# Four block-mean products in one go, 512 KB value loads, weight halves decoded in pairs, and a stage's scores in one TensorE run

## The chip, the cores and the metric

The kernel runs on one core of a Trainium2 chip. The metric is the time of one execution on the device in microseconds. The engines are called PE (TensorE, matrix products), PEld (its weight loads), DVE (VectorE), ACT (ScalarE), POOL (GpSimd) and SP (SyncE, which here issues every DMA).

## The reference

Attention in which each query sees a narrow window of keys and, beside it, one maximum of keys and one mean of values for each block of 32 positions; its result goes through a feed-forward net (FFN).

```python
# q, k, v: (B, H, S, D) = (4, 8, 768, 64); block 32, window 16; d_ff = 2048
k_sum = k.reshape(B, H, nb, block, D).max(axis=3)
v_sum = v.reshape(B, H, nb, block, D).mean(axis=3)
scores_l = where(|i - j| < window, q @ k.T / sqrt(D), -1e9)
scores_s = q @ k_sum.T / sqrt(D) + log(block)
a = softmax(concat(scores_l, scores_s))          # 1e-9 added to the sum
x = a @ concat(v, v_sum)                         # -> (B * S, H * D) = (3072, 512)
h = x @ w_in
out = (h / (1 + exp(-h))) @ w_out
```

## The kernel before

The 3,072 rows are cut into 24 attention stages of 128 rows (six for each batch) and 12 FFN chunks of 256 rows (two stages each). A chunk `c` goes through 16 slices `f` of the hidden width: `ffn1` (4 products), a tanh on ACT and a product on DVE, `ffn2` (2 outputs, `u` = 0, 1). Chunk 0 and batch 0's attention run in 32-bit floats, where one product is two passes of PE; all else is split into high and low 16-bit halves and takes three 16-bit products for one.

A planner (`Plan`) sets the order of everything. The code below registers each operation with its cost on each engine it may run on, with what it reads and writes, and with a priority; the planner sweeps over them, picks engine and place, and the program is issued in that order, engine by engine. `TUNE` holds the priorities' offsets. Where the planner sees PE idle at the start it puts in filler products (`fill`). Each engine runs its list strictly in order, so an instruction that waits holds up all behind it.

What the change and the prediction's steps touch:

- `job_qk`, `job_k0`: SP loads queries and keys (for batch 0 into `first` and `second`).
- `job_mean`: the block means of batch 0's values. For each of six tiles of 128 rows SP loads two halves `z` (120 and 96 rows of 512 columns, `v` 0 to 5, four of them into weight tiles `wr` not yet in use, two into `v0`); 12 products with a 0-or-1/32 matrix `sums` add up into 24 rows of one PSUM bank; that is copied to `vms`, and from there into the 24 free rows of each half tile.
- `job_a`: scores of a head group `m` (four for a stage; two of them share a run of products, `pair`), softmax with row maxima, exponentials and sums, and for batch 0 a transpose on PE (`turn`), for later batches a DMA transpose.
- `job_c`, `job_x`: the products of weights and values into bank 7, and its copy to `x`, the FFN's input.
- `job_load`, `job_w`: a weight slice comes as two loads (`kind` 0 of `w_in`, 1 of `w_out`) of 512 KB; ACT (`Prelu`), ACT or DVE (`last_bits`) and DVE turn its 64-bit words into 32-bit floats, and DVE takes the largest (`wm`).
- `w_scale`, `job_pair`: one scale for all weights, and each weight half as two 16-bit halves (`wh`, `wl`), which chunks 1 to 11 use.
- `job_f`: the FFN of a chunk and slice.

Score products write PSUM banks 2 to 5 at first and 6 and 3 later (`score_banks`).

Of the kernel before, what the change touches and what calls it, by code (L numbers as in the profile page):

```python
# [47 lines left out]
SETTLED = 32  # L48
SLACK = {"pe": 2500, "dve": 800, "act": 800, "pool": 800}
# [6 lines left out]
class Plan:  # L56
# [17 lines left out]
    RUSH = 140000  # L74

# [5 lines left out]
    def op(self, engines, fn, r=(), w=(), prio=0.0, cols=0, port=("dve", "pool"), fill=None):  # L81
# [11 lines left out]
        self.ops.append((engines, fn, sorted(deps), prio, cols, port, fill, dict(self.slack)))  # L93
# [20 lines left out]
    def sweep(self, prio, on, back):  # L114
# [9 lines left out]
        ready, seen, fills, filled, early, order = {}, {}, 0, self.FIRST, True, []  # L124
# [8 lines left out]
        while ready:  # L133
# [13 lines left out]
            if e == "pe" and not back:  # L147
# [8 lines left out]
                stop = self.stream(seen, t, cost, cols)  # L156
# [61 lines left out]
def local_attn_ffn(ctx: ExitStack, tc: tile.TileContext, qkT, qF, kF, v, vR, w, out):  # L218
# [15 lines left out]
    wp = ctx.enter_context(tc.tile_pool(name="wp", bufs=2 * NFT))  # L234
# [5 lines left out]
    wr = [wp.tile([P, 2 * DM], U32, name="wr") for _ in range(2 * NFT)]  # L240
# [5 lines left out]
    sums = const.tile([P, 2, NB + 4 * NTILE - 2], F32, name="sums")  # L246
    nc.vector.memset(sums, 0.0)
    for z in range(2):
        two, top = sums[:, z, NB - 2:NB], HALO + (0 if z else NB)
        nc.vector.memset(two, 1.0 / BLK)  # L250
        nc.gpsimd.affine_select(out=two, in_=two, pattern=[[-BLK, 2]], compare_op=ALU.is_ge, fill=0.0, base=-top, channel_multiplier=1)
        nc.gpsimd.affine_select(out=two, in_=two, pattern=[[BLK, 2]], compare_op=ALU.is_ge, fill=0.0, base=top + BLK - 1, channel_multiplier=-1)
    lg = const.tile([P, 1], F32, name="lg")
# [16 lines left out]
    NRAW, NP, NTT, NE, NG, NT2 = 3, 8, 12, 3, 4, 4  # L270
# [33 lines left out]
    sum_t = ring(3, [P, 2], F32, "sum")  # L304
# [30 lines left out]

    def both_ends(k):
# [34 lines left out]
    def job_scale(b, prio):  # L371
        prio += nudge("scale", b)
        for j in range(3):
            stg, key = staging()
            qf = stg[:, :2 * DM]
            plan.op({"dma": 1650}, lambda e, qf=qf, j=j: nc.sync.dma_start(out=qf, in_=qF[b - 1, :, j, :]), w=key, prio=prio)
# [9 lines left out]
        plan.op({"pe": 220}, tr, r=["qm_q", "qm_k"], w=[("bank", k)], prio=prio, cols=256)  # L386
# [29 lines left out]
    def v_scale(b, prio):  # L416
        k = sbank()
        plan.op({"pe": 110}, lambda e, k=k: nc.tensor.transpose(out=bank[k][:1, :P], in_=am_t[:, 7:8], identity=ident), r=["am4"], w=[("bank", k)], prio=prio, cols=128)
# [18 lines left out]
    def job_v(b, prio):  # L437
        prio += nudge("v", b)
        for j in range(4):
            stg, key = staging()  # L440
            vr = stg[:, :S]
            plan.op({"dma": 1230}, lambda e, vr=vr, j=j: nc.sync.dma_start(out=vr, in_=vR[b, :, j, :]), w=key, prio=prio)
# [6 lines left out]
        def tr(e, k=k):  # L449
# [10 lines left out]
    def job_qk(s, prio):  # L460
# [11 lines left out]
        plan.op({"dma": 1850}, lambda e: nc.sync.dma_start(out=raw4, in_=qkT[b, t]), w=key, prio=prio)  # L472
# [20 lines left out]
    def job_mean(prio):  # L493
        prio += nudge("mean")
        k = sbank()
        for t in range(NTILE):
            src, keys, _ = main0(t)
            for z in range(2):
                plan.op({"dma": 650}, lambda e, src=src, t=t, z=z: nc.sync.dma_start(out=src[rows0[z], z], in_=v[0, t, rows0[z], z, :]), w=[keys[z]], prio=prio)
        for t in range(NTILE):  # L500
            src, keys, _ = main0(t)
            for z in range(2):
                at = NB - 2 - 4 * t - 2 * z
                plan.op({"pe": 900}, lambda e, src=src, t=t, z=z, at=at, k=k: nc.tensor.matmul(out=bank[k][:NB], lhsT=sums[rows0[z], z, at:at + NB], rhs=src[rows0[z], z], start=(t == 0 and z == 0), stop=(t == NTILE - 1 and z == 1)),  # L504
                        r=[keys[z]], w=[("bank", k)], prio=prio, cols=2048)
# [417 lines left out]
```

## Time and profile before

| | |
|---|---|
| median of 3 runs | 617.32 us (616.46 to 617.68) |
| the profiled execution | 616.48 us |
| its span, first to last instruction | 614.4 us |
| mean granted TensorE clock | 0.997 |
| busy PE / DVE / ACT / POOL | 603.8 / 462.7 / 380.3 / 97.1 us |
| moved by DMA | 75.65 MB, mean 123 GB/s |

The time of an execution is 2.1 us more than its span. In the views of the profile a row of the timeline is: start, length, engine, line, operation, what it writes and reads, how many were merged, and in brackets how long the engine stood before it and what ended that. PE's products are pipelined, so a product's length is longer than the pitch at which products follow one another. In the view of groups the numbers behind the bar are the busy time and the mean ns of one.

### The profile page before, as it was taken

To read this page: it belongs to the slowest core of one execution; us is meant where nothing else is said; L and a number is where in the kernel's file an instruction comes from. 1 tells how busy PE (TensorE), PEld (TensorE's weight loads), DVE (VectorE), ACT (ScalarE), POOL (GpSimd) and SP (SyncE) were. 2 spreads that over 40 slices of the span, in tenths; PEclk is the share of its full clock that TensorE was granted. 3 is DMA by queue.
4 is the path that set the end of the run, shared out by engine and by line. 5 is a ranking of instruction groups with operands and counts; after the bars stand their busy time and mean duration, and the time that the engine had idled before them with its cause. 6 is when DMAs were issued, how large, how long until landed. Compare 5 with 4: busy or idle time off the path is not lost.

```text
span 614.4 us, 15092 instructions
## 1 busy us (share of the span) xinstructions
PE 603.8 (98%) x5648; PEld 398.1 (65%) x5648; DVE 462.7 (75%) x1517; ACT 380.3 (62%) x1049; POOL 97.1 (16%) x136
## 2 busy tenths in 40 slices
PE   7989999999999999999999999999999999999997
PEld 4366666666666666666666666666666666666664
DVE  4599999998997674997889965998856768833332
ACT  3799959986765664665665764655755565533333
POOL 3220000122414202004113300102123101100000
PEclk9999999999999999999999999999999999999999
DMA  9999344313733663363425761552722502200000
GB/s 236 322 400 409 136 125 123 118 49 105 197 85 76 181 194 51 113 163 101 130 60 126 185 194 33 112 161 70 180 66 38 173 19 41 71 10 1 35 1 34
DMA packets 66354, 75.65 MB, mean 123 GB/s; under 512 B 41978, under 2 KB 48122, under 8 KB 66282
## 3 DMA queue, kind: packets, MB, share of 16 engines
q1 hardware_dynamic: 66282, 74.70, 42.6%
q8 instruction: 44, 0.72, 0.5%
q14 instruction: 28, 0.23, 0.1%
HBM read 57.18 MB, written 6.29 MB: 103 GB/s over the span
## 4 chain that ended last, share of the span: by engine, by line
PE 95%; ACT 2%; SPq 1%; DVE 1%; DMA 1%; issue 0%
PE bank L747 38%; PE bank L755 38%; PE bank L744 5%; PE bank L752 5%; PE bank L577 4%; PE bank L651 2%; PE bank L504 2%; PE bank L636 1%; PE bank L609 1%; DMA wr<-in_v_dram 1%; SPq L362 1%; ACT wr L224 0%; DVE second L474 0%; ACT e L586 0%; PE bank L451 0%; PE bank L430 0%
## 5 line engine op out<-in xcount | busy, mean ns | idle before, releaser
L747 PE MATMUL bank<-x,wr 128*128 128x256 f16 x2112 | 258.1, 273 | 0.0
L747 PEld LDWEIGHTS <-wr 128*128 128x128 f16 x2112 | 204.8, 98 | 55.7 <-issue 0.9
L755 PE MATMUL bank<-wr,gh 128*128 128x512 f16 x704 | 209.9, 380 | 0.0
L761 ACT ACTIVATE t<-bank,th 128x256 f32<-128x256 f32 x176 | 82.9, 471 | 124.2 <-PE bank L747 123.9
L762 DVE SCALAR_TENSOR_TENSOR t<-t,bank 128x256 f32<-128x256 f32 x192 | 80.1, 418 | 87.7 <-ACT t L761 86.3
L755 PE MATMUL bank<-wr,gl 128*128 128x512 f16 x352 | 133.4, 379 | 0.0
L764 ACT ACTIVATE gh<-t 128x256 f16<-128x256 f32 x176 | 72.6, 414 | 58.9 <-DVE t L762 53.8
L765 DVE SCALAR_TENSOR_TENSOR gl<-t,gh 128x256 f16<-128x256 f32 x176 | 80.9, 461 | 33.7 <-ACT gh L764 32.8
L755 PEld LDWEIGHTS <-gh 128*128 128x128 f16 x704 | 65.0, 98 | 45.4 <-issue 0.3
L586 ACT ACTIVATE e<-e,mx 128x120 f32<-128x120 f32 x192 | 73.3, 386 | 4.6 <-DVE mx L583 4.0
L755 PEld LDWEIGHTS <-gl 128*128 128x128 f16 x352 | 34.4, 98 | 41.9 <-DVE gl L765 0.5
L620 DVE SCALAR_TENSOR_TENSOR first<-e,sum,first 128x120 f16<-128x120 f32 x144 | 47.7, 377 | 0.1
L583 DVE CUSTOM_DVE_ANT_0 e<-bank,masks,qsc 128x120 f32<-128x120 f32 x144 | 41.7, 337 | 0.3 <-PE bank L577 0.3
L586 ACT ACTIVATION_READ_ACCUMULATOR e<-e,mx 128x1 f32 x192 | 36.8, 192 | 0.0
L752 PE MATMUL bank<-wr,t 128*128 128x512 f32 x64 | 31.2, 602 | 0.0
L744 PE MATMUL bank<-x,wr 128*128 128x256 f32 x128 | 30.6, 383 | 0.3 <-ACT x L224 0.3
L744 PEld LDWEIGHTS bank<-x,wr 128*128 128x128 f32 x128 | 23.8, 190 | 7.7 <-issue 3.3
L231 POOL TENSOR_TENSOR first<-raw,first 128x1024 f16<-128x1024 f32 x13 | 28.2, 2174 | 0.9
L598 POOL TENSOR_SCALAR e<-e,sum 128x120 f32<-128x120 f32 x24 | 10.1, 427 | 111.3 <-DVE sum L591 103.1
L598 POOL TENSOR_SCALAR first<-e,sum 128x120 f16<-128x120 f32 x26 | 13.5, 522 | 82.2 <-DVE sum L591 40.5
L226 POOL TENSOR_SCALAR first<-raw 128x1024 f16<-128x1024 f32 x12 | 14.1, 1176 | 77.5 <-PE bank L651 77.3
L600 DVE TENSOR_SCALAR first<-e,sum 128x120 f16<-128x120 f32 x91 | 23.8, 288 | 0.8
(145 smaller groups left out, 642.6 us busy)
## 6 DMA issues: line engine op xcount, KB each, us to landing
wr<-in_w_dram SPq DMA_DIRECT2D x32, 512.0 KB
raw<-in_qkT_dram SPq DMA_DIRECT2D x18, 576.0 KB
raw<-in_v_dram SPq DMA_DIRECT2D x18, 512.0 KB
out_dram<-raw SPq DMA_DIRECT2D x24, 256.0 KB
raw<-in_kF_dram SPq DMA_DIRECT2D x12, 384.0 KB
raw<-in_qF_dram SPq DMA_DIRECT2D x9, 512.0 KB
raw<-in_vR_dram SPq DMA_DIRECT2D x12, 384.0 KB
first<-in_qkT_dram SPq DMA_DIRECT2D x6, 320.0 KB
```

Of the source, the lines that this page charges most:

```text
L231: eng[e].tensor_tensor(out=out, in0=in0, in1=in1, op=ALU.subtract)
L583: plan.op({"dve": 262 if b else 206}, lambda e, i=i: nc.vector.tensor_tensor_reduce(out=et[:, i, :], in0=sc[:, i, :NKEY], in1=mask, scale= ...
L586: plan.op({"act": 385}, lambda e, i=i: nc.scalar.activation(out=et[:, i, :], in_=et[:, i, :], func=AF.Exp, scale=-1.0, bias=mx[:, i:i + 1] ...
L620: nc.vector.scalar_tensor_tensor(out=pt[:, i, P:P + NKEY], in0=et[:, i, :], scalar=su[:, i:i + 1], in1=pt[:, i, :NKEY], op0=ALU.mult, op1= ...
L744: nc.tensor.matmul(out=h, lhsT=wi.bitcast(F32)[:, ct * P:(ct + 1) * P], rhs=x0[:, ct, :], start=(ct == 0), stop=(ct == NCT - 1))
L747: nc.tensor.matmul(out=h, lhsT=wip[:, part, ct * P:(ct + 1) * P], rhs=x[:, ct, :], start=(ct == 0 and q == 0), stop=(ct == NCT - 1 and q = ...
L752: nc.tensor.matmul(out=bank[ob[u]], lhsT=t[:, u * P:u * P + P], rhs=wo.bitcast(F32), start=opens, stop=closes)
L755: nc.tensor.matmul(out=bank[ob[u]], lhsT=g[:, u * P:u * P + P], rhs=wop[:, part, :], start=(opens and q == 0), stop=(closes and q == 2))
L761: plan.op({"act": 264 if c == 0 else 360}, lambda e: nc.scalar.activation(out=t, in_=h, func=AF.Tanh, scale=0.5 if c == 0 else th[:, 0:1]) ...
L762: plan.op({"dve": 337}, lambda e: nc.vector.scalar_tensor_tensor(out=t, in0=t, scalar=1.0, in1=h, op0=ALU.add, op1=ALU.mult), r=[("bank", ...
L764: plan.op({"act": 311}, lambda e: nc.scalar.activation(out=gh, in_=t, func=AF.Copy, scale=SHRINK), r=[("t", j)], w=[("gh", n)], prio=post)
L765: plan.op({"dve": 343}, lambda e: nc.vector.scalar_tensor_tensor(out=gl, in0=t, scalar=SHRINK, in1=gh, op0=ALU.mult, op1=ALU.subtract), r= ...
```

## The change

Six things, in short:

1. Values of batch 0 are loaded as whole tiles, six of 512 KB instead of twelve of 240 and 192 KB, and both first query tiles go ahead of them.
2. Two value tiles' four halves are multiplied as a group, each with its own 32 columns of PE and its own 32 rows of one bank (`four`); three groups add up, the result is copied out (`parts`), and one more product with a 0-or-1 matrix `gather` adds the four parts.
3. Weight slices 2 to 15 come in one load of 1 MB and are decoded with one operation for both kinds; `job_pair` makes two slices' halves in one operation.
4. All four head groups' scores of a stage are one run of products (`job_scores`); softmax goes on in pairs of head groups, with one add and one reciprocal for both. The rings `e` and `sum` are longer.
5. The first two FFN slices of chunk 0 are done in two halves of 128 rows, each waiting only for its half of `x`.
6. The planner's PSUM keys are half banks, it counts 95 ns when the tiling of PE changes, some DMA costs are lower, and `TUNE` is new.

```diff
+ALONE = 2
+HALVES = 2
...
     def job_mean(prio):
...
-            for z in range(2):
-                plan.op({"dma": 650}, lambda e, src=src, t=t, z=z: nc.sync.dma_start(out=src[rows0[z], z], in_=v[0, t, rows0[z], z, :]), w=[keys[z]], prio=prio)
-        for t in range(NTILE):
-            src, keys, _ = main0(t)
-            for z in range(2):
-                at = NB - 2 - 4 * t - 2 * z
-                plan.op({"pe": 900}, lambda e, src=src, t=t, z=z, at=at, k=k: nc.tensor.matmul(out=bank[k][:NB], lhsT=sums[rows0[z], z, at:at + NB], rhs=src[rows0[z], z], start=(t == 0 and z == 0), stop=(t == NTILE - 1 and z == 1)),
-                        r=[keys[z]], w=[("bank", k)], prio=prio, cols=2048)
-        plan.op({"act": 478, "dve": 598}, lambda e, k=k: copy(e, mean, bank[k][:NB]), r=[("bank", k)], w=["vms"], prio=prio)
+            plan.op({"dma": 1280}, lambda e, src=src, t=t: nc.sync.dma_start(out=src, in_=v[0, t]), w=keys, prio=prio + t / 8)
+        parts = raw[NRAW - 1][:, :DM], [("raw", NRAW - 1, 0)]
+        for t in range(0, NTILE, 2):
+            def four(e, t=t, k=k):
+                for i in range(4):
+                    z, at = i % 2, 4 * NTILE - 2 - 4 * (t + i // 2) - 2 * (i % 2)
+                    nc.tensor.matmul(out=bank[k][i * BLK:(i + 1) * BLK], lhsT=sums[rows0[z], z, at:at + BLK], rhs=main0(t + i // 2)[0][rows0[z], z], start=(t == 0), stop=(t == NTILE - 2))
+
+            plan.op({"pe": 1100}, four, r=main0(t)[1] + main0(t + 1)[1], w=bk(k), prio=prio, cols=2048, mode=2)
+        plan.op({"act": 478, "dve": 598}, lambda e, k=k: copy(e, parts[0], bank[k]), r=bk(k), w=parts[1], prio=prio)
+        k = sbank()
+        plan.op({"pe": 950}, lambda e, k=k: nc.tensor.matmul(out=bank[k][:NB], lhsT=gather, rhs=parts[0], start=True, stop=True), r=parts[1], w=bk(k), prio=prio, cols=2048, mode=2)
+        plan.op({"act": 478, "dve": 598}, lambda e, k=k: copy(e, mean, bank[k][:NB]), r=bk(k), w=["vms"], prio=prio)
...
+    def job_scores(s, prio):
...
+        def go(e):
+            for hp in range(4):
...
+                            nc.tensor.matmul(out=bank[both[u]][side[z], hp * P:hp * P + NKEY], lhsT=q[:, side[z]], rhs=kk[:, z * OFF:z * OFF + NKEY], start=(n == 0), stop=(n == (2 if b else 0)))
...
+        plan.op({"pe": 630 if b else 720}, go, r=need, w=bk(both[0]) + bk(both[1]), prio=prio, cols=1440 if b else 1920, mode=1)
...
+        for js in ((0,), (1,)) if s < 2 else ((0, 1),):
+            sums, su = [sum_key(j, i) for j in js for i in range(2)], su4[:, 2 * js[0]:2 * js[-1] + 2]
...
+    def job_load(f, kinds, prio):
...
+        plan.op({"dma": 1280 * n}, lambda e: nc.sync.dma_start(out=wr4[:, f, k0:k0 + n], in_=w[f][:, k0 * DM:(k0 + n) * DM].bitcast(U32).rearrange("p (k c) -> p k c", k=n)), w=keys + sides, prio=prio + nudge("wd", f, k0))
...
+        raw4 = wr4[:, f, ks].rearrange("p k (c i) -> p k c i", i=2)
+        low, top, wf = raw4[..., 0], raw4[..., 1], wr4[:, f, ks, :DM]
...
+        if i < HALVES:
+            for half in range(2):
+                cs = slice(half * P, half * P + P)
+
+                def part(e, cs=cs):
+                    for ct in range(NCT):
+                        nc.tensor.matmul(out=h[:, cs], lhsT=wi[:, ct * P:(ct + 1) * P], rhs=x0[:, ct, cs], start=(ct == 0), stop=(ct == NCT - 1))
+
+                plan.op({"pe": 900}, part, r=[("xh", z, half), ("xl", z, half)] + need, w=[("bank", k, half)], prio=i + nudge("f1", i), cols=2048, fill=fill)
...
-        for kind in range(2):
-            job_load(f, kind, f + kind / 2 - TUNE["w_dma"])
-            job_w(f, kind, f - TUNE["w_dec"] + kind)
+        for kinds in (((0,), (1,)) if f < ALONE else ((0, 1),)):
+            job_load(f, kinds, f + kinds[0] / 2 - TUNE["w_dma"])
+            job_w(f, kinds, f - TUNE["w_dec"] + kinds[0])
...
-TUNE = dict(ws=-105.5, s0=-174.0, wp=-273.5, ...
+TUNE = dict(ws=-327.75, s0=-396.25, wp=-159.5, ...
```

What the new order is, at the places on which the prediction rests. On PE, in the start-up before: the last products of the means (L504), between transposes of softmax weights (L609, `e`), and the scores of the next stage (L577, one row of eight).

```order
L504 MATMUL bank_211<-wr,sums 24x512 x2
L609 MATMUL bank_207<-ident,e_189 120x128 x2
L504 MATMUL bank_211<-v_161,sums 24x512 x2
L504 MATMUL bank_211<-v_162,sums 24x512
L609 MATMUL bank_209<-ident,e_188 120x128 x2
L504 MATMUL bank_211<-v_162,sums 24x512
L609 MATMUL bank_210<-ident,e_189 120x128 x2
L609 MATMUL bank_208<-ident,e_190 120x128 x2
```

The same place now: the last group of four (L517), the transposes (L636), the gather (L522) and the first of 16 score products.

```order
L517 MATMUL bank_190<-v_133,sums 32x512 x2
L517 MATMUL bank_190<-v_134,sums 32x512 x2
L636 MATMUL bank_188<-ident,e_164 120x128 x2
L636 MATMUL bank_189<-ident,e_165 120x128 x2
L636 MATMUL bank_189<-ident,e_169 120x128 x2
L636 MATMUL bank_186<-ident,e_166 120x128 x2
L522 MATMUL bank_190<-raw_129,gather 24x512
L584 MATMUL bank_188<-first,second 64x120
```

The two last tiles are one group, and eight transposes, four tiles' worth, now stand between it and the gather.

On ACT, at the copy of the means to `vms` before (L687 and L691 decode weights, L224 copies, L586 and L596 are softmax):

```order
L691 ACTIVATE wr<-wr 128x512
L224 COPY vms<-bank_211 24x512
L224 COPY third<-bank_208 120x256
L224 COPY wr<-vms 24x512 x3
L586 ACTIVATE e_190,sum_184<-e_190,mx_187 128x120 x2
L586 ACTIVATE e_188,sum_182<-e_188,mx_185 128x120 x2
L224 COPY wr<-vms 24x512
L224 COPY v_162<-vms 24x512
```

And now, down to the copy of `x` (L230; L731 and L735 decode):

```order
L731 ACTIVATE wr<-wr 128x512
L230 COPY third<-bank_188 120x256
L735 ACTIVATE wr<-wr 128x512
L230 COPY third<-bank_186 120x256
L731 ACTIVATE wr<-wr 128x512
L230 COPY vms<-bank_190 24x512
L735 ACTIVATE wr<-wr 128x512
L230 COPY wr<-vms 24x512 x5
L230 COPY x_170<-bank_191 128x4x128
```

All five fills that ACT does now stand in one row ahead of the copy of `x`, with a decode ahead of them.

On SP, the loads ahead of the first weights before:

```order
L464 DMA second<-in_qkT_dram 128x4x128
L499 DMA wr<-in_v_dram 120x512
L499 DMA wr<-in_v_dram 96x512
L499 DMA wr<-in_v_dram 120x512
L499 DMA wr<-in_v_dram 96x512
L464 DMA second<-in_qkT_dram 128x4x128
```

And now:

```order
L477 DMA second<-in_qkT_dram 128x4x128 x2
L511 DMA wr<-in_v_dram 128x1024 x4
L511 DMA v_133<-in_v_dram 128x1024
L511 DMA v_134<-in_v_dram 128x1024
L717 DMA wr<-in_w_dram 128x1024
```

The second query tile (L477) moved ahead of all values; the weights behind them start as single halves and go on in pairs.

More of the change, by code (lines that the diff above doesn't have):

```diff
@@ L123, in sweep @@
         shared = 0.0
-        ready, seen, fills, filled, early, order = {}, {}, 0, self.FIRST, True, []
+        ready, seen, fills, filled, early, order, mode = {}, {}, 0, self.FIRST, True, [], 0
         def arrive(i):
@@ L252, in local_attn_ffn @@
         nc.gpsimd.affine_select(out=two, in_=two, pattern=[[BLK, 2]], compare_op=ALU.is_ge, fill=0.0, base=top + BLK - 1, channel_multiplier=-1)
+    gather = const.tile([P, NB], F32, name="gather")
+    nc.vector.memset(gather, 0.0)
+    for j in range(4):
+        nc.vector.tensor_copy(out=gather[j * BLK:(j + 1) * BLK], in_=ident[j * BLK:(j + 1) * BLK, j * BLK:j * BLK + NB])
     lg = const.tile([P, 1], F32, name="lg")
@@ L334, in local_attn_ffn, with bk @@
     SBANKS, spare, PAIR = [(6,), (6, 3)], [0], (6, 3)
+    def bk(k):
+        return [("bank", k, half) for half in range(2)]
     def both_ends(k):
@@ L576, in pair @@
                                 q, kk = q0_t[s % NQ0][rows, hp], k0_t[t][rows, hp]
-                            nc.tensor.matmul(out=bank[both[u]][side[z], i * 256:i * 256 + NKEY], lhsT=q[:, side[z]], rhs=kk[:, z * OFF:z * OFF + NKEY], start=(n == 0), stop=(n == (2 if b else 0)))
-        if g % 2 == 0:
-            need = [(x, s % 2) for x in ("qh", "ql", "kh", "kl", "km2")] if b else [("q0", s % NQ0), ("k0", t), ("k0m", t)]
-            plan.op({"pe": 330 if b else 420}, pair, r=need, w=[("bank", x) for x in both], prio=prio, cols=720 if b else 960)
@@ L611, in job_a @@
-            plan.op({"pe": 230}, turn, r=er, w=[("bank", k)], prio=prio, cols=256)
-            plan.op({"act": 264, "dve": 335}, lambda e: copy(e, tt[:NKEY], tp[:NKEY, :2, :]), r=[("bank", k)], w=[ttk], prio=prio, port=())
-            return
-        pk = m % NP
-        for i in range(2):
-            plan.op({"dve": 235, "act": 296, "pool": 320}, lambda e, i=i: scaled(e, pt[:, i, :NKEY], i), r=sums + er[i:i + 1], w=[("p", pk) + (() if i else ("half",))], prio=prio)
-        def low(e):
-            for i in range(2):
-                nc.vector.scalar_tensor_tensor(out=pt[:, i, P:P + NKEY], in0=et[:, i, :], scalar=su[:, i:i + 1], in1=pt[:, i, :NKEY], op0=ALU.mult, op1=ALU.subtract)
@@ L622, in job_a @@
-        plan.op({"dve": 510}, low, r=er + sums, w=[("p", pk), ("p", pk, "half")], prio=prio)
-        plan.op({"dma": 500}, lambda e: nc.sync.dma_start_transpose(out=tt, in_=pt.rearrange("p a b -> p (a b)")), r=[("p", pk), ("p", pk, "half"), "third"], w=[ttk], prio=prio)
+                    nc.vector.scalar_tensor_tensor(out=pt[:, i, P:P + NKEY], in0=et[:, i, :], scalar=su4[:, 2 * j + i:2 * j + i + 1], in1=pt[:, i, :NKEY], op0=ALU.mult, op1=ALU.subtract)
+            plan.op({"dve": 510}, low, r=[sum_key(j, i) for i in range(2)] + [("e", n, i) for i in range(2)], w=pkeys, prio=prio)
@@ L662, in job_x @@
         if c == 0:
[L663 removed]
+            plan.op({"act": 478, "dve": 598}, lambda e: copy(e, x0[:, :, half * P:half * P + P], x3), r=bk(7), w=keys, prio=prio, port=())
             return
```

252 lines of the change are left out of this document (144 added, 108 removed).

## The prediction

> **What bounds the kernel now.** I read the page first: busy time, then the chain that ended last.
>
> ```profile
> span 614.4 us, 15092 instructions
> PE 603.8 (98%) x5648; PEld 398.1 (65%) x5648; DVE 462.7 (75%) x1517; ACT 380.3 (62%) x1049; POOL 97.1 (16%) x136
> PE 95%; ACT 2%; SPq 1%; DVE 1%; DMA 1%; issue 0%
> ```
>
> TensorE (PE) is busy for 98% and is 95% of the chain, so only two things shorten the time: PE starting its long work earlier, or PE having less to do. The stretches view, cut where the first FFN product starts (37.08), where chunk 1 starts (101.14) and where the last product ends (610.73), says where each can come from.
>
> ```profile
> 0.00:37.08 37.08, 31.17 (x252) 15.47 (x252) 22.94 (x94) 21.86 (x71) 13.08 (x40) 0.95 1.00 298
> 37.08:101.14 64.06, 64.06 (x323) 41.26 (x324) 61.43 (x152) 56.18 (x130) 2.49 (x7) 1.00 0.61 232
> 101.14:610.73 509.59, 508.55 (x5074) 341.38 (x5072) 378.33 (x1274) 301.62 (x850) 81.57 (x89) 1.00 0.37 97
> 610.73:614.40 3.67, 0.00 (x0) 0.00 (x0) 0.00 (x0) 0.69 (x1) 0.00 (x0) 0.88 0.38 143
> ```
>
> The columns are the length, then PE, PE's weight loads, VectorE (DVE), ScalarE (ACT) and GpSimd (POOL), the granted clock, the DMA share and GB/s. The first stretch is a start-up with filler products in it. In the second PE never stands, but DVE (61.43 of 64.06) and ACT (56.18) are nearly full too: whoever starts PE earlier there must also lighten those two. The third has slack on every engine but PE. PE's timeline shows the start-up:
>
> ```profile
> 11.41 1.05 PE L577 MATMUL bank<-first,second 64*64 64x120 f32 x32 [2.71 <-DMA wr<-in_v_dram]
> 12.59 4.43 PE L504 MATMUL bank<-wr,sums 120*24 120x512 f32 x6
> 24.50 2.76 PE L504 MATMUL bank<-v,sums 120*24 120x512 f32 x6
> 27.56 1.04 PE L504 MATMUL bank<-v,sums 96*24 96x512 f32 x2
> 30.46 1.15 PE L636 MATMUL bank<-third,wr 120*64 120x64 f32 x32
> 33.25 1.15 PE L636 MATMUL bank<-third,wr 120*64 120x64 f32 x32 [0.54 <-DVE x L228]
> 37.08 3.29 PE L744 MATMUL bank<-x,wr 128*128 128x256 f32 x14 [0.27 <-ACT x L224]
> ```
>
> The block means (L504: 12 products, each two passes) run from 12.59 to 28.60, and only 8.5 us after them the first FFN product starts.
>
> **Start-up, part by part.** The value loads:
>
> ```profile
> 0.00:5.00 5.00, 3.58 (x17) 2.48 (x18) 1.01 (x9) 1.28 (x1) 3.80 (x21) 1.00 0.54 144
> 5.00:10.00 5.00, 3.71 (x30) 2.88 (x27) 3.32 (x7) 0.00 (x0) 0.48 (x2) 1.00 1.14 322
> 10.00:15.00 5.00, 3.46 (x36) 1.33 (x37) 3.12 (x19) 3.44 (x16) 1.41 (x4) 0.78 1.10 240
> 15.00:20.00 5.00, 5.00 (x20) 1.27 (x22) 1.50 (x9) 2.27 (x9) 0.73 (x2) 0.88 1.03 247
> 20.00:25.00 5.00, 5.00 (x44) 1.67 (x41) 2.66 (x19) 3.19 (x15) 0.75 (x2) 1.00 1.07 294
> 40.00:50.00 10.00, 10.00 (x74) 6.55 (x72) 9.73 (x35) 9.90 (x28) 0.71 (x2) 1.00 1.03 411
> wr<-in_v_dram SPq DMA_DIRECT2D x4, 240.0 KB
> wr<-in_v_dram SPq DMA_DIRECT2D x4, 192.0 KB
> wr<-in_w_dram SPq DMA_DIRECT2D x32, 512.0 KB
> 10.08 0.69 DVE L363 TENSOR_REDUCE km<-first 128x16 f32<-128x512 f32 x1 [0.39 <-DMA first<-in_qkT_dram]
> ```
>
> Six loads of 240 KB and six of 192 KB (2.65 MB) move at 240 to 247 GB/s, 10.9 us. Six of 512 KB (3.15 MB) take 7.7 us at the 411 GB/s at which the weights, of the new shape, arrive, and 12.9 us at 243. I take the first, the row of the same shape: the last value tile lands 3.2 us earlier (bounds: 3.2 earlier, 2.0 later). By bytes: keys, two query tiles and values are 5.64 MB; 2.33 MB have moved at 10.0 (144 and 322 GB/s), 0.16 more at 322 and the values at 411 end at 18.2. A landing is seen 1.2 us later (the six key tiles, 1.97 MB, have moved at 8.9 and DVE takes the last at 10.08): 19.4. The same sum for before, 5.14 MB, is 21.3 and 22.5. The query tile that is now ahead of the values in SP's queue is counted in.
>
> The means: 12 products of two 0.43 us passes (six in 2.76, the row at 24.50) are 10.3 us of PE; now three groups of four, and one gather. If the four of a group run one after another, a group takes 8 passes, 3.44 us; if all at once, 0.86. The nearest row is L636, over 120 rows in two column groups: 32 passes of 64 columns would be 1.7 us in turn (0.43 x 64/512 each) and take 1.15 with the last one's drain. That is two at once, so I take 0.86 (bounds 0.86 and 3.44). The Trainium skill, page "TensorE: Matmul & The Clock Gate", section "Part 3: Packing small matmuls — row/col tiling", has measured 3.07 times for four row tiles and 2.38 for three column tiles, so less than four. By it a group is 3.44/3.07 = 1.12 us and my sum 0.3 us longer; no row here shows four column groups.
>
> ACT's list decides the rest; its prices:
>
> ```profile
> 28.63 0.58 ACT L224 COPY vms<-bank 24x512 f32<-24x512 f32 x1 [0.17 <-PE bank L504]
> 29.63 1.78 ACT L224 COPY wr<-vms 24x512 f32<-24x512 f32 x3
> 36.47 0.56 ACT L224 COPY x<-bank 128x512 f32<-128x512 f32 x1
> L691 ACT ACTIVATE wr<-wr 128x512 f32<-128x512 f32 x32 | 22.2, 704 | 0.7 <-DMA wr<-in_w_dram 0.7
> L377 ACT ACTIVATE raw<-raw 128x1024 f32<-128x1024 f32 x9 | 9.4, 1049 | 3.2 <-DMA raw<-in_qF_dram 3.2
> L586 ACT ACTIVATE e<-e,mx 128x120 f32<-128x120 f32 x192 | 73.3, 386 | 4.6 <-DVE mx L583 4.0
> ```
>
> After the last group (19.4 to 20.5) DVE copies the parts out; behind it in PE's order stand eight transposes (16 passes of 0.11) of stage 1, whose exponentials (the last row; 16 of them at a pitch of 0.38 from 12.4 on, and scalings) fill ACT until about 20.3, so they end at about 22.3; the gather ends at 23.4 (0.86 and 0.2 drain). Before, the last product ended at 28.6: 5.2 us. The copy of the means stands in ACT's list behind three decodes and two copies of those transposes, and ends at 24.5. A tile's two fills with means (0.6 each, ACT and POOL) let stage 0's 32 value passes run from 25.9 to 27.0. ACT has a decode and five fills (3.8 us) before it can copy x: 28.8. Stage 1's passes to 30.0; then FFN 0, cut in halves, does its first half (0.87) while ACT passes two decodes and three exponentials (0.38 each) and copies the second half of x, until 31.5. In PE's steady work this is a start at 30.7: 6.4 us earlier than 37.08. With ACT in nobody's way it would be 28.5; with serial groups 33.3.
>
> **Chunk 0.** If PE starts 6.4 us earlier, decoding must be as much earlier. DVE is busy 72.61 us and ACT 67.71 of the 76 from 25 to 101. The pairs save a fixed part for every two operations:
>
> ```profile
> 25.00:101.00 76.00, 74.34 (x440) 47.08 (x439) 72.61 (x182) 67.71 (x160) 8.40 (x17) 1.00 0.68 259
> L693 DVE SCALAR_TENSOR_TENSOR wr<-wr 128x512 uint32<-128x512 uint32 x32 | 22.1, 702 | 0.3 <-ACT wr L687 0.3
> L694 DVE TENSOR_REDUCE wm<-wr 128x1 f32<-128x512 f32 x32 | 21.2, 687 | 0.0
> L516 DVE TENSOR_REDUCE am<-wr 120x1 f32<-120x1024 f32 x4 | 4.8, 1210 | 0.0
> ```
>
> On DVE 1,024 columns cost 1.21 against twice 0.69 (a 0.17 gain); 28 such pairs in chunk 0 give 4.8 us, and the row sums done for two head groups at once some 2 more. On ACT 1.05 stands for twice 0.70: 25 pairs, 8.9 us. So 65.8 and 58.8 us of work stand in about 70 us (22.5 to 92.5): 94% of DVE, where 95.5% did not hold PE up. Bound from the other side: no gain per pair, then DVE lacks 2 to 3 us. The 1 MB weight loads come at the same 411 GB/s; the fourth pair lands near 36, and chunk 0 needs it near 48. I allow 0.8 us for waits in chunk 0 (0.5 before).
>
> **PE's own work.** From the order of instructions, behind the start of FFN 0, scores of 24 short products now stand in 18 runs of 48, not 36 of 24.
>
> ```profile
> 150.06 0.38 PE L755 MATMUL bank<-wr,gl 128*128 128x512 f16 x1
> 150.37 0.51 PE L577 MATMUL bank<-second 64*64 64x120 f16 x24
> 150.81 0.60 PE L755 MATMUL bank<-wr,gh 128*128 128x512 f16 x2
> 40.84 0.45 PE L636 MATMUL bank<-third,wr 120*64 120x64 f32 x8
> 41.23 1.12 PE L752 MATMUL bank<-wr,t 128*128 128x512 f32 x2
> ```
>
> An FFN product takes 0.215 there, so the run costs 150.81 - 150.06 - 0.215 = 0.535, of which 0.30 are its 24 starts and 0.235 entry and exit. A run of 48 is 0.235 + 0.61. Saved: 18 x 0.225 = 4.0 (between 0 and 18 x 0.235 = 4.2). The 32-bit scores go from 7 runs to 3, one half stage of them into the start-up: 1.4. The value products of batch 0 (L636: 0.39 and 0.09 of entry for a run of 8) go from 12 runs to 4: 1.7. Eight more transposes' passes at 0.11 fall behind the start: +0.9. Together -6.2. Filler is issued in the start-up alone (85 against 60 products) and costs nothing there while PE waits. The pairs of weight halves for later chunks (16 instead of 32) and single reciprocals lie on DVE and ACT, which have 131 and 208 us idle in the third stretch: nothing.
>
> **The sum.** -6.4 (start) + 0.3 (more wait in chunk 0 than before, 0.8 for 0.5) - 6.2 (PE) = -12.3, on the profiled execution of 616.48: 604.2. The median of the runs shown, 617.32, is 0.84 above that execution: 605.0.
>
> **Rivals.**
> - The start-up gain comes back in chunk 0, because decoding can't keep up (pairs that gain nothing, ACT's list late). Against it: 94%; for it: no slack on either engine. All lost: 617.3 - 6.2 = 611.1; half lost, 608.
> - The four products of a group run in turn: +2.6, 607.6.
> - The clock drops at the start of chunk 0. At 12.59 six passes took 4.43 us, at 24.50 2.76; the granted clock in between was 0.78 and 0.88, after PE had waited 2.71 us. A drop like it at 27 to 31, where PE now waits for ACT with filler between, costs 1.7: 606.7. The Trainium skill, same page, section "Part 1: The HAM clock gate (the "warmup" mystery)", says that an idle window of some 3.4 us halves the clock; the trace's 4.43 for 2.76 agrees in kind.
> - Slower: a run of 48 needs both banks of scores empty at once, where now a run of 24 follows each half. PE runs in order, so whatever a run waits stops all. PE's only wait of scores in the list of waits:
>
> ```profile
> PE bank L577 <- DMA wr<-in_v_dram: 2.7, 1, 2.7
> ```
>
>   It is in the start-up, for a load; none was for DVE. With 21 runs it takes 12.3/21 = 0.59 us a run to lose all, and 0.65 to be over 0.2% slower (618.6); DVE, at 74% in the third stretch, makes that unlikely.
> - Nothing changes: only if start-up and PE's work both fail.
>
> **Chances.** Likeliest, 605.0, own range 602 to 607: 0.62. Start-up given back: 0.17. Serial groups: 0.08. Clock: 0.06. Slower: 0.04. Same within 0.2% (1.2 us, about what a measurement of this kernel can tell from no change): 0.03. Faster is the sum of the first four, 0.93. The range 601.5 to 610.5 takes in all but the worst of the second and the last two; its low end is the start at 28.5 with no wait more in chunk 0 (602.5) and 1 us for the unknown.
>
> **What the changed profile would show.** The last value load landed at 19 to 20; groups of four of 8 passes in about 1.1 us each (3.4: the serial rival); the gather's end near 23.4; first FFN product near 30, its second half near 31.5, no clock below 1.00 from 25 on; chunk 1 starting at 92 to 94 (97 or later: given back); 18 runs x48 of scores at 0.84 to 0.87 us between FFN products; no wait of PE for DVE above 1 us behind chunk 0. Wrong would be most of all a later start of FFN 0 through ACT's list, or waits of PE on decoded weights.

## The result and the profile after

The changed kernel takes 613.42 us (median of 13 runs, 610.38 to 616.36), the kernel before, run beside it, 617.68 (13 runs, 616.46 to 621.16). The ratio is 0.9923, with a 95% interval of 0.9901 to 0.9945: 0.8% faster, a third of the 12.3 us forecast, and outside the range. The profiled execution took 613.2 us.

The page after: span, busy time, the chain that ended last.

```profile
span 611.5 us, 14976 instructions
PE 593.8 (97%) x5687; PEld 402.1 (66%) x5687; DVE 442.9 (72%) x1342; ACT 381.1 (62%) x1028; POOL 102.1 (17%) x162
PE 79%; DVE 7%; DMA 6%; ACT 4%; issue 1%; SPq 1%; POOL 0%; ACTq 0%
```

PE's share of the chain was 95% and is 79%: DVE, transfers and ACT now hold the end on stretches where PE held it. The stretches, cut at the same events as before (first FFN product, start of chunk 1, last product; columns as there: length, PE, weight loads, DVE, ACT, POOL, clock, DMA share, GB/s):

```profile
0.00:30.71 30.71, 25.44 (x288) 16.78 (x288) 20.66 (x93) 17.86 (x57) 13.96 (x43) 0.94 0.96 345
30.71:97.75 67.04, 62.98 (x327) 42.06 (x325) 60.32 (x117) 51.86 (x103) 3.62 (x11) 0.97 0.66 249
97.75:607.68 509.93, 505.35 (x5078) 343.27 (x5076) 361.89 (x1134) 310.68 (x869) 84.48 (x109) 1.00 0.36 95
607.68:611.48 3.80, 0.00 (x0) 0.00 (x0) 0.00 (x0) 0.69 (x1) 0.00 (x0) 0.78 0.36 138
```

PE's own work is the instructions in its order, each by the spacing that its kind has in the trace where nothing waits. What a stretch holds beyond it is waiting (idle time, slow clock, rests). How the spacings are taken moves some 0.4 us between work and waiting:

| us | before | after | difference |
|---|---|---|---|
| first FFN product starts | 37.08 | 30.71 | -6.37 |
| PE's work in chunk 0 | 63.58 | 60.96 | -2.62 |
| waiting in chunk 0 | 0.48 | 6.08 | +5.60 |
| PE's work behind it | 507.84 | 503.95 | -3.89 |
| waiting behind it | 1.74 | 5.98 | +4.24 |
| tail | 3.70 | 3.80 | +0.10 |
| span | 614.42 | 611.48 | -2.94 |

The two gains are all there, 6.4 and 6.5 us. 9.8 us of new waiting stand against them, where I had allowed 0.3; 0.8 of the 9.8 lie between the two halves of FFN 0, which the forecast had counted to the start. The list of PE's waits gives two places most of it (us in total, times, longest; first of 37 to 101 us, then of 101 on):

```profile
PE bank L795 <- DVE t L823: 2.3, 1, 2.3
PE bank L443 <- DVE sc L439: 0.6, 1, 0.6
...
PE bank L689 <- DMA third<-first: 2.5, 2, 1.9
PE bank L443 <- DVE sc L439: 1.2, 1, 1.2
```

**The end of chunk 0.** PE's timeline, and the window of slow clock behind the wait:

```profile
81.75 1.88 PE L803 MATMUL bank<-wr,t 128*128 128x512 f32 x4
83.87 1.13 PE L803 MATMUL bank<-wr,t 128*128 128x512 f32 x2 [0.24 <-DVE t L823]
85.22 0.38 PE L761 MATMUL bank<-ident,wx 128*1 128x128 f32 x2 [0.23 <-DVE wx L756]
87.90 4.35 PE L795 MATMUL bank<-x,wr 128*128 128x256 f32 x12 [2.29 <-DVE t L823]
```

```profile
84.13:87.54 3.41, 1.25 (x4) 0.12 (x3) 1.12 (x3) 2.18 (x5) 0.00 (x0) 1.00 0.59 179
87.54:90.96 3.42, 3.06 (x7) 2.52 (x8) 2.49 (x6) 0.00 (x0) 0.00 (x0) 0.50 0.55 181
90.96:94.37 3.41, 3.41 (x15) 2.36 (x14) 1.66 (x8) 1.48 (x3) 0.00 (x0) 1.00 0.46 151
```

PE waits for t (L823), which waits for a tanh (L822), and that stands in ACT's list behind other work. Follow it back in ACT's timeline, then in DVE's:

```profile
79.05 0.84 ACT L369 ACTIVATE raw<-raw 128x768 f32<-128x768 f32 x1 [3.60 <-DVE km L367]
...
83.74 1.06 ACT L390 ACTIVATE raw<-raw 128x1024 f32<-128x1024 f32 x1 [1.24 <-DMA raw<-in_qF_dram]
...
85.97 1.06 ACT L390 ACTIVATE raw<-raw 128x1024 f32<-128x1024 f32 x1 [1.08 <-DMA raw<-in_qF_dram]
...
87.03 0.36 ACT L822 ACTIVATE t<-bank 128x256 f32<-128x256 f32 x1
```

```profile
70.99 2.34 DVE L738 TENSOR_REDUCE wm<-wr 128x2 f32<-128x1024 f32 x2
73.24 0.41 DVE L823 SCALAR_TENSOR_TENSOR t<-t,bank 128x256 f32<-128x256 f32 x1
73.57 4.59 DVE L738 TENSOR_REDUCE wm<-wr 128x2 f32<-128x1024 f32 x4
78.07 0.94 DVE L367 TENSOR_REDUCE km<-raw 128x24 f32<-128x768 f32 x1
```

The tanh is behind two sums over q of the next batch (L390). Their tiles are loaded into staging tiles that the sums over k (L369) had to leave first (SyncE waited for L369 twice, 7.2 us in all, and gave the two loads out from 80.0 on), and those wait for the maxima over k (L367), which stand in DVE's list behind six maxima over weight pairs (L738). DVE does not rest from the first of the six to these maxima over k. From 26.2 to the reduction of all weight maxima (L756 at 84.98; in the kernel before L705, at 86.75) it works nearly all the time, in both kernels, after (first) and before:

```profile
26.20:84.98 58.78, 56.06 (x364) 38.47 (x364) 57.02 (x103) 50.09 (x103) 7.67 (x17) 1.00 0.74 290
```

```profile
26.20:86.75 60.55, 58.89 (x390) 38.34 (x389) 59.04 (x150) 55.88 (x136) 7.92 (x17) 1.00 0.76 290
```

So the weight maximum came 1.8 us earlier, not 6.4, and PE, early and with less to do, ran up against DVE's list.

**The value products at 168.** PE's timeline, and SyncE's queue ahead of it:

```profile
167.47 0.57 PE L689 MATMUL bank<-third,first 120*64 120x64 f16 x24
168.63 0.38 PE L689 MATMUL bank<-third,first 120*64 120x64 f16 x12 [0.60 <-DMA third<-first]
170.87 0.38 PE L689 MATMUL bank<-third,first 120*64 120x64 f16 x12 [1.86 <-DMA third<-first]
```

```profile
161.72 1.54 SPq L549 DMA_DIRECT2D raw<-vms  x2
163.38 5.25 SPq L657 DMA_TRANSPOSE third<-first  x4
168.69 1.54 SPq L549 DMA_DIRECT2D raw<-vms  x2
```

Four transposing DMAs are given out in 5.25 us, 1.35 from one to the next. The planner lays them out at 0.50 each.

### The profile page after: what moved, and what is told of

Same layout as the page of the kernel before. It is cut to its first block, busy times and chain, and to the rows that moved or that the text cites. A ratio compares the mean times of both kernels' runs of the same rounds, so it can differ in the third digit from the quotient of the medians.

```text
span 611.5 us, 14976 instructions
## 1 busy us (share of the span) xinstructions
PE 593.8 (97%) x5687; PEld 402.1 (66%) x5687; DVE 442.9 (72%) x1342; ACT 381.1 (62%) x1028; POOL 102.1 (17%) x162
## 4 chain that ended last, share of the span: by engine, by line
PE 79%; DVE 7%; DMA 6%; ACT 4%; issue 1%; SPq 1%; POOL 0%; ACTq 0%
PE bank L798 36%; PE bank L806 35%; DVE wm L738 3%; PE bank L689 3%; PE bank L584 2%; DMA wr<-in_w_dram 2%; ACT wr L735 1%; DVE wr L737 1%; PE bank L803 1%; DMA wr<-in_v_dram 1%; PE bank L795 1%; DMA raw<-in_qF_dram 1%; DMA raw<-in_qkT_dram 1%; DVE t L823 1%; ACT wr L731 1%
## 5 line engine op out<-in xcount | busy, mean ns | idle before, releaser
L822 ACT ACTIVATE t<-bank,th 128x256 f32<-128x256 f32 x176 | 82.7, 470 | 105.3 <-PE bank L798 104.6
L823 DVE SCALAR_TENSOR_TENSOR t<-t,bank 128x256 f32<-128x256 f32 x192 | 79.9, 416 | 91.7 <-ACT t L822 91.0
L806 PEld LDWEIGHTS <-gh 128*128 128x128 f16 x704 | 66.6, 98 | 45.0
L623 POOL TENSOR_SCALAR first<-e,sum 128x120 f16<-128x120 f32 x53 | 24.1, 463 | 130.2 <-DVE sum L616 58.8
L795 PE MATMUL bank<-x,wr 128*128 128x256 f32 x112 | 28.2, 398 | 2.3 <-DVE t L823 2.3
L237 POOL TENSOR_TENSOR first<-raw,first 128x1024 f16<-128x1024 f32 x12 | 25.8, 2149 | 23.9 <-ACT first L230 23.2
L795 PEld LDWEIGHTS bank<-x,wr 128*128 128x128 f32 x112 | 21.9, 200 | 8.8 <-DVE t L823 2.8
L737 DVE SCALAR_TENSOR_TENSOR wr<-wr 128x1024 uint32<-128x1024 uint32 (+1 forms) x18 | 19.8, 1106 | 1.8 <-ACT wr L735 1.4
L621 ACT ACTIVATE first<-e,sum 128x120 f16<-128x120 f32 x52 | 18.5, 384 | 3.6 <-DVE sum L616 2.5
```

The source lines that it names most:

```text
L623: nc.gpsimd.tensor_scalar(out=out, in0=src, scalar1=by, scalar2=0.0, op0=ALU.mult, op1=ALU.add)
L795: nc.tensor.matmul(out=h, lhsT=wi[:, ct * P:(ct + 1) * P], rhs=x0[:, ct, :], start=(ct == 0), stop=(ct == NCT - 1))
L806: nc.tensor.matmul(out=bank[ob[u]], lhsT=g[:, u * P:u * P + P], rhs=wop[:, part, :], start=(opens and q == 0), stop=(closes and q == 2))
L822: plan.op({"act": 264 if c == 0 else 360}, lambda e: nc.scalar.activation(out=t, in_=h, func=AF.Tanh, scale=0.5 if c == 0 else th[:, 0:1]) ...
L823: plan.op({"dve": 337}, lambda e: nc.vector.scalar_tensor_tensor(out=t, in0=t, scalar=1.0, in1=h, op0=ALU.add, op1=ALU.mult), r=bk(k), w=[ ...
```

## The experiments

**1. Less work for VectorE, order kept.**

```diff
-... in_=wf.bitcast(F32), axis=AX.X, op=ALU.max ...
+... in_=wf.bitcast(F32)[:, :, :DM // 2], axis=AX.X, op=ALU.max ...
```

> The changed kernel, its order of instructions kept on every engine; each maximum over the joined weights reads only the first half of its columns (so the weight scale comes from half of the weights), which takes about 8.5 us of work out of VectorE's list ahead of the weight scale: 14 reductions of 1.13 us become about 0.6, 4 of 0.56 become about 0.3. Theory A (VectorE's full list holds the end of chunk 0; it worked 57.0 of the 58.8 us from 26.2 to the reduction of all maxima at 85.0): PE's waits at 83 to 88 (0.40, 0.39, 2.46 us) and the half clock from 87.5 to 91.0 (1.6 us) go, chunk 1 starts near 93 instead of 97.7, and the whole is 4.5 to 5 us below the changed kernel's 613.2 to 613.4: about 608.6. Rival B (the wait is for ScalarE, or for the loads of q that ScalarE stands on, whatever VectorE does): the wait at 85 to 88 stays, the time is within 1 us of 613.3. Rival C (the weights come too late): the same as B.

Measured: 609.61 us (609.35 to 610.13), ratio to before 0.9873 (0.9860 to 0.9886). PE's list of waits has none of the three rows from 83 to 88, the clock there is 1.00, and chunk 0 is 62.05 us long for 67.04:

```profile
30.14:92.19 62.05, 60.78 (x326) 41.13 (x324) 52.82 (x117) 51.89 (x103) 6.69 (x11) 1.00 0.71 271
```

3.8 us of the 4.5 to 5 show in the medians; in this profile the slow clock came behind the value products instead (0.50 from 166.7 to 170.2). Theory A holds, B and C fall. The control is the same edit in the kernel before:

> The kernel before, in its own order, with the same edit: each of its 32 maxima reads half of the columns (32 reductions of 0.69 become about 0.4 us, some 9 us less on VectorE). Theory A: in the kernel before, PE was never held in chunk 0 (64.06 us with 63.6 us of work), so its lighter VectorE gains at most 0.5 us: 616.5 to 617.3. Rival: VectorE held it too, in stalls too short to show as waits: 2 us or more below it.

Measured: 617.45, ratio 1.0001 (0.9990 to 1.0013). In the kernel before, DVE was as full and held nobody.

**2. Fewer transposing DMAs, order kept.**

```diff
-... lambda e, tt=tt, pt=pt: nc.sync.dma_start_transpose(...) ...
+... lambda e, tt=tt, pt=pt, j=j: None if j else nc.sync.dma_start_transpose(...) ...
...
-... rhs=tt[:NKEY, 2 * j + part, side[z]] ...
+... rhs=parts[i - i % 2][0][:NKEY, 2 * j + part, side[z]] ...
```

> The changed kernel, order kept, but of the transposing DMAs every second one is left out (value products then read the tile of the head pair beside it). Theory D: SyncE gives out a transposing DMA every 1.35 us, and now the four of a stage stand one behind the other in its queue (issued 163.38, 164.75, 166.11, 167.42, last landing 170.83), so the value products wait 0.79 and 2.05 us at 167.8 and 168.8. With two of them, the last is given out near 166.1 and lands near 168.5: both waits go, about 2.7 us, 610.6. Rival E: they land late because three loads of 512 to 576 KB were given out at 157.9 to 159.7, just ahead of them, or because VectorE's low halves are late: the waits keep at least half of their 2.84 us.

Measured: 609.57 (607.99 to 610.74), ratio 0.9870 (0.9853 to 0.9887). Both waits before L689 are gone, though the three large loads stand where they stood: theory D. The 3.8 us are more than the 2.7 expected: in this profile the wait at 85 was still there (2.0 us), but fell so that the clock stayed at 1.00.

> The changed kernel, order kept, with both edits at once: maxima over half of the columns, and every second transposing DMA left out. If the two places are all that stands between the change and its forecast, and each costs its wait and, where the wait falls so, a window of half clock: 609.6 (maxima alone) less the 2.4 us of waits before value products that were left there at 162 to 165, and less 1.7 us of half clock behind them: 605.5, the forecast of 605.0 within 1 us. Rival (the waits are interchangeable: one gone, another takes its place): 608 or more.

Measured: 605.18 (604.81 to 605.45), ratio 0.9792 (0.9768 to 0.9816). That is the forecast time, so these two places hold what lies between forecast and result. The edits take more out than the two waits (half of the maxima's columns, 36 of 72 transposing DMAs), so this shows where the time went, not that a kernel with all its work could get it back; experiment 5 does.

**3. Filler in the wait.** Twenty filler products behind the two transposes of L761.

> The changed kernel, order kept, with 20 filler products (128x256, 0.11 us each, results unused) behind the two transposes of the weight maxima on TensorE, where it stands for 2.46 us from 85.4 on. Theory: the wait itself stays (it is for VectorE's list), but TensorE is not idle in it and the granted clock stays at 1.00 instead of 0.5 from 87.5 to 91.0, which cost 1.6 us (seven passes at 0.43 us for 0.216): 611.7. Rival: the clock falls all the same, or the filler delays products that could have run: 613.3 or more.

Measured: 613.21 (612.05 to 614.23), ratio 0.9930 (0.9917 to 0.9943): no gain, the rival's time. In the profiled execution, the slowest of the six (614.23), chunk 0 did get 1.6 us shorter (65.44) and its clock stayed at 1.00; but there the wait at 167 was followed by two slow windows:

```profile
165.00:168.35 3.35, 1.33 (x41) 0.91 (x39) 2.67 (x8) 2.38 (x6) 1.62 (x3) 1.00 0.45 94
168.35:175.17 6.82, 6.16 (x77) 4.11 (x77) 1.83 (x9) 2.33 (x4) 3.17 (x2) 0.50 0.43 68
```

**4. One part undone, the planner's table unchanged.** Two misses.

> The changed kernel with its start-up undone alone: twelve value loads of 192 and 240 KB and twelve products one after the other for the block means, as in the kernel before; scores, weight pairs and halves of the first FFN products stay, and the planner lays out a new order. Theory A (what the start-up gained was given back in chunk 0, for VectorE): FFN 0 starts about 6 us later, near 36 to 37, chunk 0 is about 4 to 5 us shorter, and the whole is 613 to 615.5. Rival (the start-up's gain is in the total and something else ate the rest): 6.4 us above, 619.7.

> The changed kernel with one part undone alone: every weight tile loaded and decoded by itself (32 loads of 512 KB, operations of 512 columns); a new order follows. By starts in the trace a pair's join is 1.135 us against twice 0.599, its maximum 1.129 against twice 0.596, ScalarE's decode 1.05 against twice 0.565. So single operations cost VectorE 28 x 0.063 = 1.8 us more and ScalarE about 25 x 0.08 = 2.0 us more ahead of the weight scale. Theory A: 1 to 2.5 us slower than the changed kernel, 614.5 to 616. By the durations that the prediction used (1.21 against twice 0.69): 4.8 us slower, 618. Rival (long operations of 1.1 us in VectorE's list make short urgent ones late): faster than 613.3.

Measured: 625.83 and 624.63, ratios 1.0130 (1.0102 to 1.0157) and 1.0106 (1.0074 to 1.0138), above every theory. The edits change durations, the planner answers with other orders, and its priorities do not fit them: in the first FFN 0 starts at 39.96, later than in the kernel before; in the second, waits stand all over (2.40 us at 205, 2.26 at 290, 1.77 at 500). They tell nothing of the parts.

**5. Another order, no work left out.** The planner's prices are set to the trace's, and the table of priorities searched anew.

```diff
-plan.op({"dma": 500}, lambda e, tt=tt, pt=pt: nc.sync.dma_start_transpose( ...
+plan.op({"dma": 1350}, lambda e, tt=tt, pt=pt: nc.sync.dma_start_transpose( ...
...
-plan.op({"pe": 1800 if c == 0 else 1312}, ffn1 ...
+plan.op({"pe": 1728 if c == 0 else 1312}, ffn1 ...
...
-TUNE = dict(ws=-327.75, s0=-396.25, wp=-159.5, wm=343.0, km=395.25, ...
+TUNE = dict(ws=4.75, s0=-147.75, wp=-696.5, wm=426.75, km=113.75, ...
```

> The changed kernel with another order of the same operations: the planner's prices of TensorE's work (chunk 0 FFN products 1.728 and 0.86 us instead of 1.8 and 0.9, a run of scores 0.66 for 0.63, value products 0.785 for 0.77) and of SyncE's (a transposing DMA 1.35 for 0.50, two copies of the means 1.75 for 1.40) are those that the trace of the changed kernel shows, and the table of priorities was searched anew under them. Theory A1 (VectorE has too much work ahead of the weight scale, in any order): the waits at the end of chunk 0 stay, only the 2.8 us before the value products can go: 609 to 611. Theory A2 (the work fits, but stood in an order laid out with the wrong prices): most of the 12.1 us of waits behind the first FFN product go, to about 2 to 3: 603 to 605.

Measured: 604.27 (604.10 to 606.58), ratio 0.9789 (0.9762 to 0.9817): theory A2, and faster than both kernels. The start, chunk 0 and the rest, and PE's largest waits:

```profile
0.00:29.58 29.58, 25.08 (x282) 15.92 (x282) 20.89 (x94) 17.74 (x57) 13.23 (x42) 1.00 0.97 348
29.58:93.37 63.79, 62.26 (x330) 41.26 (x327) 61.08 (x120) 53.71 (x103) 2.81 (x8) 1.00 0.68 256
93.37:598.57 505.20, 504.01 (x5076) 342.46 (x5074) 358.26 (x1139) 305.98 (x865) 87.21 (x107) 1.00 0.38 97
```

```profile
PE bank L443 <- DVE sc L439: 0.8, 1, 0.8
PE bank L803 <- DVE t L823: 0.6, 1, 0.6
```

DVE has as much to do (61.08 of 63.79 us), and PE waits 4.1 us behind its first FFN product (63.79 + 505.20 less 564.91 of work) for 12.1, where theory A2 had 2 to 3. So VectorE's work fits; in the changed kernel it stood in an order that made PE wait. What it costs to undo each part, under an order of its own, searched for as long:

> The kernel before, its work as it was, with what the tuned kernel got: the planner's prices as traces show them (chunk 0 FFN products 1.728 and 0.86, a run of 24 scores 0.534, value products 0.973, a transposing DMA 1.35, two copies of the means 1.75) and the table of priorities searched anew for the same time. Theory O (what the tuned kernel gained over the changed one, 9.1 us, is order alone and has nothing to do with the change): the kernel before gains about as much, 608 to 609. Theory P (order can only give back waits): behind its first FFN product the kernel before has 2.2 us of waits in all, so it gains at most that and some of its start-up: 613.5 to 616.

> The tuned kernel with the start-up undone alone (twelve loads and twelve products one after the other), its own priorities searched for as long. It replaces the run of the same undoing whose order did not fit. If the start-up's gain stays in the total where the order fits: 604.3 + 6.4 = 610.7. Theory A (VectorE's list, 61.1 of 63.8 us full in chunk 0 of the tuned kernel, takes most of it): 605.5 to 608.

> The tuned kernel with single weight tiles (loads of 512 KB, operations of 512 columns), its own priorities searched for as long. By starts, VectorE has 1.8 us and ScalarE 2.0 us more ahead of the weight scale, where the tuned kernel's chunk 0 leaves VectorE 2.7 us: 604.3 to 606. By the durations the prediction used, 4.8 us more on VectorE, 2.1 beyond the 2.7: 606.5 or more. Rival (pairs are in the way of urgent short operations): below 604.

> The tuned kernel with a stage's scores as two pieces of TensorE work again, one for each two head groups, its own priorities searched for as long; in the order that came out 20 runs of 24 stand, 8 of 48 are still whole. A run costs 0.849 us against twice 0.534 by starts. Theory (the saving is TensorE's own work, which nothing hides): 10 x 0.22 = 2.2 us for the 16-bit scores and up to 1 us for the 32-bit ones, 606.5 to 607.5. Rival (halves let work start earlier and pay for it): 604.3 or less.

| tuned, with undone | us | ratio to before | interval | first FFN product | from there to the last |
|---|---|---|---|---|---|
| nothing | 604.27 | 0.9789 | 0.9762 to 0.9817 | 29.58 | 568.99 |
| the start-up | 610.22 | 0.9887 | 0.9870 to 0.9905 | 35.39 | 568.85 |
| weight pairs | 609.45 | 0.9873 | 0.9855 to 0.9890 | 29.83 | 573.47 |
| scores in one run | 609.79 | 0.9875 | 0.9850 to 0.9899 | 32.89 | 569.79 |
| everything (kernel before) | 616.89 | 0.9985 | 0.9971 to 0.9999 | 37.97 | 572.35 |

The kernel before gains 0.15% from a new order: theory P, and less than even its band. The start-up's gain stays whole (5.95 us, theory A falls here): what DVE took away in the changed kernel was the order's doing. Undoing weight pairs costs 5.2 us, not the 1.8 that spacing gives. Chunk 0 was not the place (61.66 us long), but three waits for DVE of 1.1 to 1.2 us that end at 116, 154 and 188; how far the search left them there stays open. Undoing the run of scores costs 5.5 us, 2.2 to 3.2 expected, and 3.3 of it is a later start. The start-up has three runs of 16 passes of 32-bit scores there, where the tuned kernel has one of 32; that they account for the 3.3 isn't shown. The three parts add up to 16.6 us and undoing everything costs 12.6: each row is the outcome of one search, so a row is a part's worth only to within some microseconds.

**6. Prices or table?**

> The changed kernel with the tuned kernel's prices in the planner, but the changed kernel's own table of priorities. If the wrong prices are what cost the waits, the order now avoids them: 604 to 607. If the table of priorities is what matters (it had been set for an order under other prices), the waits stay, elsewhere: 610 to 616.

> The tuned kernel's table of priorities, but the changed kernel's own prices in the planner. If prices matter (a transposing DMA at 0.50 where SyncE takes 1.35 us above all), the value products wait for transposed tiles again, 2 us or more, and the time is 608 or more; if the table alone does it, 604 to 606.

Measured: 617.58 and 621.08, ratios 1.0004 (0.9991 to 1.0017) and 1.0060 (1.0037 to 1.0082). The first lies above both of its bands, the second where prices matter. With the right prices no wait for a transposing DMA is left, but one of 2.3 us for t at the end of chunk 0, and several of up to 1.1 for DVE and ACT elsewhere. With the old prices under the new table the value products wait for them again, three times, 1.6 us in all (2 or more expected), but more is lost on five waits for DVE's `gl`, 5.3 us in all. So neither half does it alone: here the table served only with the prices under which it was searched.

Neither of these two orders leaves the right output. Filler products write the PSUM bank of the first FFN slice after its products and before ACT has read them: with the right prices four of L326 at 33.75, with the old ones five of L790 at 31.58, between the slice's two halves. The planner's keys don't hold filler back from a bank in use, and since the first slices are cut in halves there is room for filler behind a half. The two runs tell what an order costs; they are not kernels to use.

## Why the prediction was right or wrong

- **Start-up: right, 0.8 late.** Groups of four take 1.06 us each, so all four run at once (3.44 in turn). They start at 16.00, 18.24 and 20.15, the last waiting for its tile (forecast landing 19.4, group's end 20.5, found 21.8). From the gather on every step comes 0.4 to 0.9 after its forecast: gather's end 23.8 for 23.4, value passes of stage 0 from 26.3 for 25.9, of stage 1 from 29.6 to 30.8, first half of FFN 0 at 30.71 for 30.0, the second at 32.40 for 31.5. Counted as the forecast did, with the wait between the halves, the start gained 5.6 us for 6.4.

```profile
16.00 1.06 PE L517 MATMUL bank<-wr,sums 120*32 120x512 f32 x8
18.24 1.07 PE L517 MATMUL bank<-wr,sums 120*32 120x512 f32 x8
20.15 1.64 PE L517 MATMUL bank<-v,sums 120*32 120x512 f32 x8
22.73 1.04 PE L522 MATMUL bank<-raw,gather 128*24 128x512 f32 x2
30.71 1.16 PE L817 MATMUL bank<-x,wr 128*128 128x128 f32 x8
32.40 1.83 PE L817 MATMUL bank<-x,wr 128*128 128x128 f32 x14 [0.54 <-ACT x L230]
```

- **PE's own work: right.** 6.5 us less for 6.2; runs of 48 stand at 0.85 with entry and exit (0.84 to 0.87 forecast), and none waits for its banks in the changed kernel.
- **Chunk 0: the step that failed.** The forecast allowed 0.8 us of waits there, and 6.1 were found. Both the prices and the comparison were wrong. The prices were the durations in the rows (1.21 against twice 0.69 on DVE, 1.05 against twice 0.70 on ACT). But an instruction's row ends after the next one has started. By starts (before, then after, both ACT's timeline):

```profile
55.43 0.66 ACT L687 ACTIVATE wr<-wr 128x512 uint32<-128x512 uint32 x1
55.99 0.66 ACT L691 ACTIVATE wr<-wr 128x512 f32<-128x512 f32 x1
56.56 0.67 ACT L687 ACTIVATE wr<-wr 128x512 uint32<-128x512 uint32 x1
```

```profile
55.30 1.15 ACT L731 ACTIVATE wr<-wr 128x1024 uint32<-128x1024 uint32 x1
56.35 1.17 ACT L735 ACTIVATE wr<-wr 128x1024 f32<-128x1024 f32 x1
57.42 0.35 ACT L822 ACTIVATE t<-bank 128x256 f32<-128x256 f32 x1
```

  ACT: 1.05 to 1.07 against twice 0.565, a gain of 0.07 a pair (the forecast's 1.05 was the duration of another kind, L377; a pair's decode has a row of 1.16). DVE's maxima before:

```profile
61.55 0.69 DVE L694 TENSOR_REDUCE wm<-wr 128x1 f32<-128x512 f32 x1
62.14 0.69 DVE L693 SCALAR_TENSOR_TENSOR wr<-wr 128x512 uint32<-128x512 uint32 x1
```

  The next row starts 0.59 after the maximum (the median of all 32 is 0.596). After, four maxima reach from 73.57 to the next start at 78.07, 1.13 each: a gain of 0.063. So the pairs gave DVE 28 x 0.063 = 1.8 us instead of 4.8, and ACT 2 instead of 8.9. The comparison, "94% of DVE, where 95.5% did not hold PE up", sets side by side averages of a chunk; what counted was the order within it: six maxima ahead of a row that ACT, a load and then a tanh stood on. With 8.5 us less in DVE's list the wait and its slow clock were gone (experiment 1); with nothing less in it and another order, too (experiment 5). Whether the 3 us of relief that the pairs fell short of would have been enough in the changed kernel's order, no run shows.
- **The rival** "the start-up gain comes back in chunk 0" is half of what happened (5.6 of 6.4 us, with the 0.8 between the halves of FFN 0); its 0.17 was far too low. That its 611.1 comes near the 613.4 is luck: it has none of the 4.2 us of new waiting behind chunk 0.
- **The step that was missing:** SyncE's queue. Nothing in the sum prices the transposing DMAs. The value products at 168 wait for the later ones of four that are given out in a row from 163.38: 2.5 us of waits, and in the profiles of experiments 1 and 3 slow windows behind them. In the kernel before there are such rows too, but the stage's first four start at 160.5, 163.9 and (two) 165.8; the tuned kernel gives out six in a row from 156.1, and PE doesn't wait for them. So it is when they are given out that counts here. The sign "no wait of PE for DVE above 1 us behind chunk 0" was missed by one of 1.2 (a scale, L443); for waits on DMAs the forecast had no sign.
- **The clock rival** had the right price, 1.7, and the wrong place.

## What to carry to other kernels

Price a full in-order list by the distance between starts, not by rows' durations; here that turned 4.8 us of relief into 1.8. When a change lets the main engine start earlier or do less, walk back in the lists of the engines it waits for, to the row that ends last, before counting the gain: a list that held nobody at 95% held PE for 5 us once PE was 6 us early. And where a planner lays the order out, a part can only be judged, by doing or undoing it, under an order searched for it: the same parts measured 11 to 12 us under an ill-fitting order and 5 to 6 under fitting ones.

## What the runs showed of the hardware

- A wait of two to three microseconds can cost another 1.7: the granted clock is 0.50 for windows of 3.41 us, when PE was busy for too little of the window ahead (1.25 of 3.41 in the row at 84.13). Whether it happens depends on where the wait falls. With half of the transposing DMAs a wait of 2.0 us at 85 was shared by two windows (2.36 and 2.01 us of work, from 82.32 and 85.74), and the clock stayed at 1.00; in the changed kernel one of 2.3 halved it. Laid out on each trace's own grid, all 12 windows at full clock with at most 1.5 us of work (ahead of the last product) were followed by 0.50, all with 1.7 or more by 1.00, and 1.65 went both ways. Out of a slow window more is needed: 2.75 us of work in the one at 168.35 of experiment 3 were followed by a second. The Trainium skill, page "TensorE: Matmul & The Clock Gate", section "Part 1: The HAM clock gate (the "warmup" mystery)", has the window of 3,413 ns and that it runs free of the kernel. The traces agree: the slow windows of the changed kernel start at 12.45 and 87.54, 22 such windows apart, and in the kernel before the first starts at 12.79. The Trainium skill asks for an idle window; here 2.2 idle us of one (3.41 less 1.25) were enough.
- The spread of the changed kernel's runs goes with the clock: its four fastest (610.38 to 611.42) have a mean granted clock of 0.996 to 1.000, its three slowest (615.42 to 616.36) of 0.988 to 0.991. With both waits gone the four runs lie within 0.64 us, at 0.996 to 1.000.
- SyncE needs 1.35 us to give out a transposing DMA of 128x512 16-bit elements (5.25 us for the four at 163.38), where a load of 512 KB takes it 0.3 to 0.4.
